# Attention visits, loads and inner factors moved within the slots of a paired attention-and-MLP kernel

## The chip, the cores and the metric

The kernel runs on one core of a Trainium2 chip. The metric is device time in microseconds (us), the median of several executions. Before the change it is 1418.35 us (three runs, 1418.15 to 1419.4). The engines are called as in the profile: PE (TensorE: matrix products), PEld (its weight loads), DVE (VectorE), ACT (ScalarE), POOL (GpSimd), SP (the queue from which all DMAs of the main part are issued).

## The reference

What is computed, cut to what matters:

```python
# 8 batches, 12 heads, 448 rows, 64 columns a head
q_n, k_n = rmsnorm(q, g_q), rmsnorm(k, g_k)
scores = q_n @ k_n.T / sqrt(64)
attn = exp(scores - max) ; attn = attn / (sum(attn) + 1e-9)
x = (attn @ v)                # to (8*448, 768)
h = x @ w_in                  # w_in 768 x 2048
g = h - tanh(h)
out = g @ w_out               # w_out 2048 x 768
```

All is float32 in the kernel's matrix products.

## The kernel before, in words

Attention is cut into 48 steps: a step s is one pair of heads of one batch, so a batch has six steps. The MLP is cut by batch. Both of its layers are multiplied in Strassen's manner (seven products in place of eight), so there are sums before and after the products; the seven are called p (or q, one level further in) and stand in the order 1, 5, 6, 2, 3, 7, 4. From batch 2 on, two batches make a pair: the first hidden layer of the pair (28 products of six matmuls), two "outer products" of the output layer, the second hidden layer, five more outer products. An outer product is itself seven inner products q of four matmuls with 224 columns, and a last, large one of eight matmuls with 448 columns.

The order of all work is written out by hand; nothing reorders it. Each engine takes its instructions in the order of recording, and waits for other engines at semaphores. The MLP is a generator, `stream`, which records one matmul at a time with whatever follows a finished product. `run(ns)` lets the stream go on for a given nominal time (0.373 us for a matmul of 224 columns). `slot(s)` places one step's attention: first the **visit** (`visit`), a burst of small matmuls in which the values of step s and the scores of step s+1 alternate; then 14 **points** in `work`, with a fifteenth part of the slot's nominal time of MLP between each two. At the points stand what step s+1 needs before its visit (sums of the exponentials: `add`, `fold`, `gather`, `spread_sums`, `widen_sums`, `turn_sums`), what step s+2 needs (`scale_blocks`, `turn_blocks`), and what step s+3 needs (`square_blocks`, `norm_blocks`, `meet_blocks`). In a hidden layer a slot holds 42 matmuls. `AHEAD_NS` is the MLP work that the slots of batch 2 record beyond the end of the single layers; as later slots hold whole fractions of a layer, it fixes where all later visits stand behind a layer's end: 18 matmuls behind it.

What the steps of the prediction touch:

- Products go to three banks in turn (`mm_bank`); products 2, 3 and 7 add to the banks of 1, 5 and 6. A product can start when the bank's last content has been read by DVE or ACT: L898 (ACT, product 1), L900, L902, L910, L906/L907, L914 (DVE: products 5, 6, 3, 7, 4), L878 with L879 (tanh on ACT and the subtraction, product 2), in the outer products L1156 and L1162 (ACT), L1089 (DVE), and L1096 (ACT) for the large product.
- A tanh (L878) of products 3, 7 and 4 is recorded one product later (`late["todo"]`) and its subtraction (L879) goes to POOL.
- The inner factors `u` (`inner_sum`, L1040) are differences of blocks of g, formed on POOL. For the first outer product of each part they are recorded beside the hidden layer, at the products that `due_sums` names; for the others within the outer product before. `outer_sum` (L1032) forms the outer ones on DVE.
- `divide` (L751, L752, L756) stands at the end of a visit: ACT copies one half of the values, DVE adds the other and multiplies by the reciprocal sums. Then DVE has `add` (L595), `add_third` (L601), `add_last` (L608), `fold` (L705), `fold_rest` (L712), `scale_blocks` (L528), `turn_blocks` (L538, L542). ACT follows with g on kT (L543), `gather` (L720, two halves of four copies), the squares (L499), `widen_sums` (L735). POOL raises to -1/2 (`power_blocks`, L521) right after the visit, and forms the sums of x (`x_sums_later`, L787).
- The q and k rows of a step are loaded by eight DMAs (`load_blocks`, L495) into one of two buffers (`qk_nat`); `scale_blocks` is the buffer's last reader. v is loaded by four DMAs after a visit. Weights go through a ring of six tiles (`ring_load`), five ahead.
- The scores of a visit go to three other banks in turn, so the second wave of scores waits until the exponential p_last (L570), the first of the visit, has read its bank.

Of the kernel before, what the change touches and what calls it, by code (L numbers as in the profile page):

```python
# [21 lines left out]
ENGINE_NS = 2.4  # L22
# [122 lines left out]
def bounded_path(tc, ctx, q, k, v, moe_w_in, moe_w_out, out, g_col, ident, ones, half_ones, neg_half, early):  # L145
# [30 lines left out]
    HS = S // 2  # L176
    HC, HF = CD // 2, CF // 2
    SETS = CF // 4
# [28 lines left out]
    def bank_of(name):  # L207

        turns[name] += 1
        return banks[name][turns[name] % len(banks[name])]  # L210
# [6 lines left out]
    def qk_rows():  # L217
        return nat.tile([P, 4 * NCH * D], F32, name="qk_nat", bufs=2)
# [241 lines left out]
    def turn(s, tk, tq):  # L460

        rr, n = normed.pop(s), early["n"]
        kn = loaded.pop(("k", s))
        for c in range(NCH):
            nc.tensor.transpose(tk[:, c * P : (c + 1) * P], kn[:, c].rearrange("p h d -> p (h d)"), ident)
        kT = qkp.tile([P, S], F32, name="kT")
        nc.scalar.mul(kT, tk[:, :S], g_col)
        for c in range(NCH):
            nc.tensor.transpose(
                tq[:, c * CP : (c + 1) * CP], n[:, c].rearrange("p h d -> p (h d)"), ident[:CP, :CP]  # L470
            )
        qT = qkp.tile([P, S], F32, name="qT")
        nc.scalar.copy(out=qT, in_=tq[:, :S])
        turned[s] = rr, kT, qT
# [12 lines left out]
    def load_blocks(s):  # L487
        b, hp = steps[s]
        t = loaded["qk", s] = qk_rows()[:, : 2 * S].rearrange("p (i j d) -> p i j d", i=2, j=NJ)
        for i, src in enumerate((q, k)):  # L490
            for h in range(2):
                rows = src[b, 2 * hp + h].rearrange("(j t) (m d) -> m t j d", t=BL, d=BL)
                for m in range(2):
                    r = (2 * h + m) * BL
                    nc.sync.dma_start(out=t[r : r + BL, i], in_=rows[m])  # L495

    def square_blocks(s):
        sq = normed["sq", s] = late["blocks"].tile([P, 2, NJ, BL], F32, name="qk_n", bufs=1)
        nc.scalar.activation(  # L499
            sq.rearrange("p i j d -> p (i j d)"), loaded["qk", s].rearrange("p i j d -> p (i j d)"), AF.Square  # L500
        )
# [7 lines left out]
    def meet_blocks(s):  # L509

        mine, other = normed["rr", s]
        for g in range(P // BL):
            own, met = slice(g * BL, (g + 1) * BL), slice((g ^ 1) * BL, ((g ^ 1) + 1) * BL)
            nc.vector.tensor_tensor(out=other[own], in0=mine[own], in1=mine[met], op=ALU.add)  # L514
        nc.vector.tensor_scalar(out=other, in0=other, scalar1=1.0 / D, scalar2=1e-6, op0=ALU.mult, op1=ALU.add)  # L515
        normed["rr", s] = other
# [16 lines left out]
    def turn_blocks(s, i):  # L533

        n = normed[s][:, i].rearrange("p j d -> p (j d)")
        if i == 0:
            qT = qkp.tile([P, S], F32, name="qT")
            nc.vector.transpose(out=qT, in_=n)  # L538
            turned[s] = qT
            return  # L540
        kT = qkp.tile([P, S], F32, name="kT")
        nc.vector.transpose(out=kT, in_=n)  # L542
        nc.scalar.mul(kT, kT, g_col)  # L543
        turned[s] = None, kT, turned[s]
        del normed[s]

    def sc_bank():
        return bank_of("sc")
# [34 lines left out]
    def full(s):  # L583

        return probs[s, 0][:, :, 0], probs[s, 1][:, :, 1], probs[s, 2][:, :, 0]

    def add(s, now=True):

        if s <= NP + NP // 2:
            sums[s] = []  # L590
            return
        t = early["sum"]
        sums[s] = [t]
        p = full(s)
        nc.vector.tensor_tensor(out=t, in0=p[0], in1=p[1], op=ALU.add)  # L595
        if now:
            add_third(s)
# [5 lines left out]
    def add_last(s):  # L603
        last = probs[s, KF][:, :, 0]
        for n in range(2 if sums[s] else 0):
            t = sums[s][0]
            part = t[n * KR : (n + 1) * KR, :, n * HS : (n + 1) * HS]
            nc.vector.tensor_tensor(out=part, in0=part, in1=last[n * KR : (n + 1) * KR], op=ALU.add)  # L608
# [107 lines left out]
    def gather(s, h):  # L716

        acc, part = whole[s], whole["part", s]
        for g in range(P // BL):
            nc.scalar.copy(  # L720
                out=acc[h * BL : (h + 1) * BL, g], in_=part[g * BL : (g + 1) * BL, h * NJ : (h + 1) * NJ]
            )

    def spread_sums(s):

        acc = whole[s]
        total = whole[s] = late["blocks"].tile([2 * BL, NJ], F32, name="sum_all")
        nc.vector.reduce_sum(total, acc.rearrange("p g j -> p j g"), axis=AX.X)
        nc.vector.reciprocal(total, total)

    def widen_sums(s):

        total = whole[s]
        wide = whole[s] = late["blocks"].tile([2 * BL, NJ, BL], F32, name="sum_w")
        nc.scalar.copy(out=wide, in_=total[:, :, None].to_broadcast([2 * BL, NJ, BL]))  # L735
# [33 lines left out]
    def x_sums_later(s, second):  # L769
        b, hp = steps[s]  # L770
        for c in {(HC + 1, 1): (0,), (HC + 1, 2): (1,), (HC + 2, 0): (2,)}.get((hp, second), ()):
            x_sums(b, (c,), range(4), nc.gpsimd)
# [82 lines left out]
    def hidden(b):  # L855
# [25 lines left out]
        def done_with(j):  # L881
# [11 lines left out]
            def use(p, bank):  # L893
                v = view(bank)
                if b >= PAIRED:
                    beside_hidden(b, j, p)
# [145 lines left out]
    def beside_hidden(b, j, p):  # L1042

        second = b % 2
        if second:
            due_sums = {(SETS // 2, 6): (0,), (SETS - 1, 4): (1,)}
        else:
            due_sums = {(SETS // 2, 6): (0,), (SETS - 1, 7): (1,), (SETS - 1, 4): (2, 3)}
        for i in due_sums.get((j, p), ()):
            inner_sum(3 if second else 1, i)  # L1050
        if second and j and p in (1, 6):
            outer_sum(p // 6, j - 1)
# [243 lines left out]

    H_NS = 4 * HS / ENGINE_NS * 7 * 6 * SETS
    O_NS = 4 * HS / ENGINE_NS * 7 * HC * HF
    AHEAD_NS = 4 * HS / ENGINE_NS * 18
    OUTER_NS = 4 * HS / ENGINE_NS * (7 * HF // 2 + 2 * HF)  # L1300

    def gap_ns(s):
# [3 lines left out]
        if s < 3 * NP:  # L1306
            return (H_NS + O_NS + AHEAD_NS) / (4 * NP)
        n = (s - 3 * NP) % (2 * NP)
        return (H_NS / 16, OUTER_NS * SOON / 8, H_NS / 16, OUTER_NS * (len(OUTER) - SOON) / 8)[(n > 3) + (n > 5) + (n > 9)]

    def has(s):
        return 0 <= s < NS
# [69 lines left out]
    def slot(s):  # L1382

        gap = gap_ns(s)
        av = av_banks
        if has(s + 1):
            scores(s + 1, KF)
        if s < FOLDED:
            last_values(s, av)
            totals(s, sc_bank())  # L1390
            divide(s, values(s, av))
            for c in range(KF):
                scores(s + 1, c)
        else:
            visit(s, av)
        if has(s + 2):
            load(s + 2, "v")
        rows, ahead, following = has(s + 2), has(s + 3), has(s + 1)
        folded = following and s + 1 >= FOLDED
        first = s + 3 == TURNED  # L1400
        scaled = rows and not first
        if scaled:
            power_blocks(s + 2)
        work = (
            ((following, lambda: add(s + 1, False)), (first, lambda: turn(s + 2, sc_bank(), sc_bank()))),
            (
                (following, lambda: add_third(s + 1)), (first, lambda: load_blocks(s + 3)),
                (True, lambda: x_sums_later(s, 0)),
            ),
            ((following, lambda: add_last(s + 1)), (first, lambda: load_blocks(s + 4))),  # L1410
            ((folded, lambda: fold(s + 1)),),
            ((folded, lambda: fold_rest(s + 1)), (True, lambda: x_sums_later(s, 1))),
            ((scaled, lambda: scale_blocks(s + 2)),),
            ((scaled, lambda: turn_blocks(s + 2, 0)), (folded, lambda: gather(s + 1, 0))),
            ((scaled, lambda: turn_blocks(s + 2, 1)), (folded, lambda: gather(s + 1, 1))),
            ((folded, lambda: spread_sums(s + 1)), (ahead, lambda: square_blocks(s + 3))),
            (
                (has(s + 4) and not first, lambda: load_blocks(s + 4)), (True, lambda: x_sums_later(s, 2)),
                (folded, lambda: widen_sums(s + 1)),
            ),  # L1420
            ((ahead, lambda: norm_blocks(s + 3)),),
            ((ahead, lambda: meet_blocks(s + 3)),),
            ((folded, lambda: turn_sums(s + 1)),),
            (),
        )
        for point in work:
            run(4 * gap / (len(work) + 1))
            for wanted, fn in point:
                if wanted:
                    fn()  # L1430
        run(4 * gap / (len(work) + 1))
# [10 lines left out]
    for s in range(2 * NP, NS):  # L1442
        slot(s)
# [346 lines left out]
```

## Time and profile before

| what | value |
|---|---|
| median of three runs | 1418.35 us |
| profiled execution | 1419.13 us, span 1417.3 us |
| busy: PE / DVE / POOL / ACT | 1338.8 / 1063.2 / 720.1 / 525.6 us |
| mean granted PE clock | 0.98 |
| a visit, and the time between two visits in a hidden layer | 5.50 us and 16.02 us |
| bytes read and written in HBM | 205 and 46 MB |

A span is the time from the first to the last instruction. A row of a timeline gives start, duration, engine, line, operation, result and operands, and in brackets the engine's idle time before it with what ended it. In a table of windows the columns are the window, its length, the busy time of PE, PEld, DVE, ACT and POOL with the number of instructions, the granted PE clock, the share of the DMA engines and GB/s. PE works on two records a matmul, so six matmuls are twelve records.

### The profile page before, as it was taken

How to read it: one execution, taken by the hardware profiler on the slowest of the kernel's cores; microseconds unless marked ns; L12 is line 12 of the kernel's file. 1: busy time of each engine (PE TensorE's matmuls, PEld its weight loads, DVE VectorE, ACT ScalarE, POOL GpSimd, SP SyncE). 2: the span in 40 equal slices, each digit the busy share in tenths (PEclk: the TensorE clock that was granted, in tenths of full speed). 3: DMA queues.
4: the chain of work that ended last, by engine and by line, in shares of the span. 5: the costliest groups of instructions: out<-in, count | busy, mean ns of one | idle time of the engine just before them, and what ended most of it. 6: DMA issues, size and time to landing. Idle time of an engine off the chain costs nothing.

```text
span 1417.3 us, 29026 instructions
## 1 busy us (share of the span) xinstructions
PE 1338.8 (94%) x11336; PEld 1044.0 (74%) x11336; DVE 1063.2 (75%) x1558; ACT 525.6 (37%) x1194; POOL 720.1 (51%) x409
## 2 busy tenths in 40 slices
PE   7988999999999997999899998899899999899996
PEld 3467844498889885688677896578777798689885
DVE  4999989668747888689788588689888688633564
ACT  7856555333333533344211444234412244301100
POOL 4756665257652447334774236624487224712651
PEclk9999999999999998999999999999999999999998
DMA  7878889889997654566455856365644775345554
GB/s 173 194 204 255 265 232 251 242 269 323 303 272 224 172 152 117 112 173 173 112 143 138 207 143 166 88 147 171 170 116 127 149 190 169 107 132 177 165 148 84
DMA packets 371685, 253.52 MB, mean 179 GB/s; under 512 B 282196, under 2 KB 310228, under 8 KB 371540
## 3 DMA queue, kind: packets, MB, share of 16 engines
q1 hardware_dynamic: 371536, 251.57, 65.2%
q8 instruction: 92, 1.51, 0.4%
q14 instruction: 53, 0.43, 0.1%
q10 hardware_dynamic: 4, 0.00, 0.0%
HBM read 205.23 MB, written 46.27 MB: 177 GB/s over the span
## 4 chain that ended last, share of the span: by engine, by line
PE 71%; DVE 14%; POOL 5%; issue 3%; DMA 3%; SPq 1%; ACT 1%; ACTq 0%; DVEq 0%; POOLq 0%
PE mm L831 32%; PE mm L1082 17%; PE sc L564 8%; PE mm L1246 5%; PE sc L630 5%; POOL u L1040 2%; DVE xT L756 1%; PE sc L668 1%; DVE qk_n L528 1%; PE sc L618 1%; POOL tt L787 1%; DVE rows L601 1%; DVE rows L608 1%; POOL rr_other L521 1%; DVE gT L1032 1%
## 5 line engine op out<-in xcount | busy, mean ns | idle before, releaser
L831 PE MATMUL mm<-xT,w_f 128*128 128x224 f32 x1296 | 265.9, 355 | 0.9 <-DVE s L900 0.9
L831 PEld LDWEIGHTS mm<-xT,w_f 128*128 128x128 f32 x1296 | 243.0, 190 | 21.0 <-issue 10.6
L564 PE MATMUL sc<-qT,kT 64*32 64x448 f32 (+1 forms) x3072 | 214.1, 500 | 3.1 <-ACT p_last L570 1.9
L521 POOL TENSOR_TENSOR rr_other<-rr_other,neg_half 128x28 f32<-128x28 f32 x33 | 160.6, 4868 | 102.8 <-DVE rr_other L515 102.8
L831 PE MATMUL mm<-tt,w_f 128*128 128x224 f32 x1044 | 208.0, 353 | 2.9 <-DVE acc L1089 2.7
L831 PEld LDWEIGHTS mm<-tt,w_f 128*128 128x128 f32 x1044 | 197.1, 190 | 5.1 <-DVE acc L1089 3.4
L1082 PE MATMUL mm<-u,w_f 128*128 128x224 f32 x672 | 146.5, 372 | 35.5 <-issue 16.7
L879 POOL TENSOR_TENSOR gT<-s,th 128x448 f32<-128x448 f32 x60 | 75.0, 1250 | 199.2 <-ACT th L878 199.2
L1082 PEld LDWEIGHTS mm<-u,w_f 128*128 128x128 f32 x672 | 132.6, 200 | 42.5 <-issue 26.7
L1082 PE MATMUL mm<-gT,w_f 128*128 128x224 f32 (+1 forms) x480 | 138.4, 442 | 2.1 <-ACT s L1156 2.1
L1082 PEld LDWEIGHTS mm<-gT,w_f 128*128 128x128 f32 x480 | 94.6, 199 | 42.6 <-issue 38.6
L564 PEld LDWEIGHTS sc<-qT,kT 64*32 64x32 f32 x3072 | 70.8, 106 | 70.8 <-issue 51.7
L879 POOL TENSOR_TENSOR g<-s,th 128x448 f32<-128x448 f32 x36 | 47.2, 1317 | 148.9 <-ACT th L878 140.9
L630 PE MATMUL sc<-p,v_nat 64*32 64x448 f32 x1120 | 111.4, 536 | 0.0
L1082 PE MATMUL mm<-g,w_f 128*128 128x224 f32 (+1 forms) x360 | 103.1, 439 | 3.5 <-DVE s L1089 3.0
L720 ACT COPY sum_g<-sum 32x14 f32<-32x14 f32 x280 | 56.3, 201 | 121.2 <-DVE sum L712 115.6
L878 ACT ACTIVATE th<-s 128x448 f32<-128x448 f32 x96 | 55.1, 575 | 120.0 <-DVE s L910 95.1
L1082 PEld LDWEIGHTS mm<-g,w_f 128*128 128x128 f32 x360 | 69.9, 197 | 34.0 <-issue 27.8
L752 DVE TENSOR_TENSOR xT<-xT,sc 128x448 f32<-128x448 f32 x32 | 19.8, 620 | 100.1 <-PE sc L564 79.3
L570 ACT ACTIVATE p<-sc 128x448 f32<-128x448 f32 x132 | 71.9, 545 | 50.6 <-PE sc L564 37.8
L1246 PE MATMUL mm<-gT,w_out 128*128 128x448 f32 x192 | 74.3, 542 | 0.0
L514 DVE TENSOR_TENSOR rr_other<-rr_mine 32x28 f32<-32x28 f32 x132 | 70.5, 534 | 3.9
(187 smaller groups left out, 2402.3 us busy)
## 6 DMA issues: line engine op xcount, KB each, us to landing
w_f<-w_in SPq DMA_DIRECT2D x196, 384.0 KB, 3.7
w_f<-w_inner SPq DMA_DIRECT2D x63, 512.0 KB, 3.6
w_f<-w_out SPq DMA_DIRECT2D x42, 512.0 KB, 4.6
w_raw<-in_moe_w_out_dram SPq DMA_DIRECT2D x16, 768.0 KB, 5.4
w_in<-w_out SPq DMA_DIRECT2D x21, 384.0 KB, 5.0
qk_nat<-in_q_dram SPq DMA_DIRECT2D x132, 56.0 KB, 2.2
qk_nat<-in_k_dram SPq DMA_DIRECT2D x132, 56.0 KB, 2.3
g<-w_out SPq DMA_DIRECT2D x14, 512.0 KB, 5.2
```

What stands on the lines that cost most here:

```text
L514: nc.vector.tensor_tensor(out=other[own], in0=mine[own], in1=mine[met], op=ALU.add)
L521: nc.gpsimd.tensor_tensor(out=mine, in0=mine, in1=neg_half[:, :1].to_broadcast([P, 2 * NJ]), op=ALU.pow)
L564: nc.tensor.matmul(tiles[h][i * BL : (i + 1) * BL, :n], lhsT=kT[r, c * P + at : c * P + at + BL], rhs=qT[r, first : first + n], start=True ...
L570: nc.scalar.activation(p[:, h, c if c < 2 else 0, :], tiles[h][:, :n], AF.Exp, scale=1.0 if rr is None else rr[:, 0, 2 * c + h : 2 * c + h ...
L630: nc.tensor.matmul(av[g][i * BL : (i + 1) * BL, :S], lhsT=v_nat[keys, h, c, m * BL : (m + 1) * BL], rhs=p[keys, h], start=first, stop=True ...
L720: nc.scalar.copy(out=acc[h * BL : (h + 1) * BL, g], in_=part[g * BL : (g + 1) * BL, h * NJ : (h + 1) * NJ])
L831: nc.tensor.matmul(bank[:, f * HS : (f + 1) * HS], lhsT=w[:, c * width + f, :], rhs=moving[p](c), start=(first and f == 0 and c == 0), sto ...
L878: nc.scalar.activation(th, h, AF.Tanh, bias=0.0, scale=1.0)
L879: eng.tensor_tensor(out=g[:, rows, cols], in0=h, in1=th, op=ALU.subtract)
L1040: nc.gpsimd.tensor_tensor(out=u, in0=a, in1=z, op=ALU.subtract)
L1082: nc.tensor.matmul(bank[:, :n], lhsT=w(i), rhs=mv, start=(first and i == 0), stop=(i == len(moving) - 1), skip_group_check=not first,)
L1246: nc.tensor.matmul(bank[:, :S], lhsT=w_out_row(f, n // HC)[:, n % HC * P : (n % HC + 1) * P], rhs=g[:, f, :], start=(f == 0), stop=(f == C ...
```

## The change

Four things move; no instruction is added, and none is removed.

1. `AHEAD_NS` holds 8 matmuls in place of 18: all visits from step 18 on stand 10 matmuls nearer to the layers' ends, and so do their points.
2. The q and k loads: in place of step s+4 at the tenth point of slot s, step s+3 at the first point.
3. In a pair's first hidden layer the second inner factor of the first outer product is recorded with the last two, at the last product (4), in place of the one before (7).
4. The two gathers go one point later each, `widen_sums` two points later, and `x_sums_later(s, 2)` stays at the tenth point.

```diff
-            due_sums = {(SETS // 2, 6): (0,), (SETS - 1, 7): (1,), (SETS - 1, 4): (2, 3)}
+            due_sums = {(SETS // 2, 6): (0,), (SETS - 1, 4): (1, 2, 3)}
...
-    AHEAD_NS = 4 * HS / ENGINE_NS * 18
+    AHEAD_NS = 4 * HS / ENGINE_NS * 8
...
-            ((following, lambda: add(s + 1, False)), (first, lambda: turn(s + 2, sc_bank(), sc_bank()))),
+            (
+                (following, lambda: add(s + 1, False)), (first, lambda: turn(s + 2, sc_bank(), sc_bank())),
+                (ahead and not first, lambda: load_blocks(s + 3)),
+            ),
...
-            ((following, lambda: add_last(s + 1)), (first, lambda: load_blocks(s + 4))),
+            ((following, lambda: add_last(s + 1)),),
...
-            ((scaled, lambda: turn_blocks(s + 2, 0)), (folded, lambda: gather(s + 1, 0))),
-            ((scaled, lambda: turn_blocks(s + 2, 1)), (folded, lambda: gather(s + 1, 1))),
-            ((folded, lambda: spread_sums(s + 1)), (ahead, lambda: square_blocks(s + 3))),
-            (
-                (has(s + 4) and not first, lambda: load_blocks(s + 4)), (True, lambda: x_sums_later(s, 2)),
-                (folded, lambda: widen_sums(s + 1)),
-            ),
+            ((scaled, lambda: turn_blocks(s + 2, 0)),),
+            ((folded, lambda: gather(s + 1, 0)), (scaled, lambda: turn_blocks(s + 2, 1))),
+            ((folded, lambda: gather(s + 1, 1)), (ahead, lambda: square_blocks(s + 3))),
+            ((folded, lambda: spread_sums(s + 1)), (True, lambda: x_sums_later(s, 2))),
             ((ahead, lambda: norm_blocks(s + 3)),),
-            ((ahead, lambda: meet_blocks(s + 3)),),
+            ((folded, lambda: widen_sums(s + 1)), (ahead, lambda: meet_blocks(s + 3))),
```

## The prediction

> **What bounds the kernel now.** I read the page first (PE, TensorE, busy 94% of the span), then the busy time by windows, then PE's waits from 450 to 1250 us, where the paired batches run beside attention, and last the timeline around the long waits.
>
> ```profile
> 450.00:1250.00 800.00, 756.26 (x6486) 601.17 (x6471) 632.18 (x923) 287.07 (x712) 401.88 (x208) 0.97 0.56 146
> 563.80:569.80 6.00, 5.97 (x18) 5.49 (x19) 2.39 (x9) 0.18 (x2) 4.31 (x1) 0.55 0.72 190
> 1250.00:1408.00 158.00, 155.72 (x727) 137.06 (x726) 79.99 (x114) 15.23 (x31) 62.98 (x35) 1.00 0.56 152
> ```
>
> The columns are busy time on PE, PEld, DVE, ACT, POOL, then the granted clock. PE is without work for 43.7 us of the 800. The second row is the stretch after one long wait: PE is busy at 0.55 of its clock, so (1 - 0.55) x 6.0 = 2.7 us more go. The last row is the end, without attention: nothing to win there.
>
> ```profile
> PE mm L1082 <- issue: 16.7, 3, 6.5
> PE mm L1082 <- POOL u L1040: 10.9, 2, 5.5
> PE mm L1082 <- DVE s L907: 7.0, 5, 2.1
> PE mm L831 <- DVE acc L1089: 2.7, 2, 1.4
> PE mm L1082 <- ACT s L1156: 2.1, 2, 1.9
> ```
>
> These are PE's waits in the same stretch: total, times, longest. They stand at the layers' ends. Three follow the end of a pair's first hidden layer (528.3, 867.9, 1208.9: 2.1 us each; the second pair adds 1.9), three the first two outer products (6.5, 6.5, 3.7), two the second hidden layer (5.5, 5.4), two the start of that layer (1.35, 1.3). After the eight longest the clock is down: windows of 6 us give 0.72 four times and 0.51 to 0.55 four times, 4 x 1.7 + 11.3 = 18 us. Waits and clock, some 61 us, are the ceiling.
>
> The longest wait in the timeline:
>
> ```profile
> 547.16 3.00 DVE L601 TENSOR_TENSOR rows<-rows,p_full 128x896 f32<-128x896 f32 x1
> 550.68 4.33 DVE L608 TENSOR_TENSOR rows<-rows,p_last 64x448 f32<-64x448 f32 x2
> 549.16 2.94 POOL L1040 TENSOR_TENSOR u<-gT 128x896 f32<-128x896 f32 x1
> 552.06 2.46 POOL L1040 TENSOR_TENSOR u<-gT,u 128x896 f32<-128x896 f32 x1
> 560.30 0.67 ACT L543 ACTIVATE kT<-kT,g_col 128x448 f32<-128x448 f32 x1 [1.77 <-DVE kT L542]
> 563.21 0.52 ACT L1096 COPY acc<-mm 128x448 f32<-128x448 f32 x1
> 563.83 1.08 PE L1082 MATMUL mm<-u,w_f 128*128 128x224 f32 x2 [6.50 <-issue]
> 526.28 2.94 DVE L528 TENSOR_TENSOR qk_n<-qk_nat,rr_other 128x896 f32<-128x896 f32 x1
> 530.43 1.37 PE L1082 MATMUL mm<-u,w_f 128*128 128x224 f32 x6 [2.12 <-DVE s L907]
> 679.00 1.80 POOL L879 TENSOR_TENSOR g<-s,th 128x448 f32<-128x448 f32 x1 [5.68 <-ACT th L878]
> 683.00 1.49 PE L1082 MATMUL mm<-u,w_f 128*128 128x224 f32 x3 [5.46 <-POOL u L1040]
> ```
>
> DVE's sums after a visit, 1.08 and 2 x 0.64 us in a quiet slot, take 3.00 and 4.33 beside POOL's inner factors. DVE is then late with kT (L542), ACT waits for it in its queue, and behind it stand the gathers, the squares and L1096, which empties the bank that PE's q=6 needs. "issue" hides this: PE starts 0.1 us after L1096 ends. At 528 scaling (L528, else 1.08) takes 2.94 beside POOL's factor, and L906/L907, behind it, empty PE's bank late. At 677 a tanh stands behind kT and the gathers on ACT, then its shrink and the second factor on POOL.
>
> **Visits 10 matmuls earlier.** A matmul of the stream takes 0.381 us (42 in the 16.02 us between two visits), a visit 5.50 us of PE. At a layer's end the visit now falls between q=5 and q=6. The products that waited at 557, 590 and 677 thus stand behind 5.5 us of other PE work, while the queue that they waited for starts 3.8 us sooner: 9.3 us of cover against 6.5, 1.35 and 5.5. The wait at 873 (L1156 after squares and widening on ACT) is covered alike. I count all of these as gone.
>
> **Factors later.** In the first layer u1 leaves the middle of DVE's burst (q=7) for the last use, where three factors of 2.1 us follow each other. L528 goes back to 1.08, L907 ends 1.9 us sooner, and the burst itself stands 3.8 us earlier: the waits of 2.1 are gone.
>
> First pair: 2.1 + 1.7 clock, 6.5 + 2.7, 1.35, 5.5 + 2.8: 22.7 us. Second: 22.7 + 1.9 + about 1 clock = 25.6. Third: 2.1 + 1.7 + 3.7 + 1.7 = 9.2. Together 57.5. The 1.0 us at 734 and 1075 stay.
>
> What is late next, from visits' ends on, with the durations of the quiet slot at 496 to 508 us (sixteen DVE instructions, 11.3 us up to L542; the same number after the change):
>
> - First hidden layer, j=2: u0 stays at q=6, but this is now 10 matmuls after the visit, in the burst. A DVE instruction waits 1.9 us; L902 and L879 are then late by 0.2 to 0.5, and the next visit's second wave by 1.0. 1.5 x 3 pairs = 4.5.
> - First outer product: shrinks to about 17.4 us after the last visit's end, then u1 to u3 to 23.7. The next visit ends at 21.5, so L756 waits for u3, one shrink (1.1) slips between, and q=5's L1089, now behind the visit in DVE's order, ends 4.9 us after the visit. q=3 needs its bank after 3.05: 1.85. The large product waits 1.0 for q=3's sum behind L705. 2.85 x 3 = 8.6.
> - Second outer product: 0.5 x 2, from the x sums on POOL beside L595 and L601 (1.41, 1.36 instead of 1.09).
> - Second hidden layer: its outer sum (1.02) moves from ahead of the visit into the burst. ACT then reaches the exponential p_last 2.2 us after a visit starts (now 0.75), ends it at 2.55, and the second wave of scores needs its bank at 1.9: 0.65 x 3 visits x 2 pairs = 3.9.
> - Third outer product: u3 is recorded behind the power (L521, 4.78 us), where it stood ahead: about 1.0 x 2.
>
> In all 20; one half-clock window in some places brings it to 23.5.
>
> [...] By the rows alone (L756 at 0.62) q=3 would wait 0 to 0.7, 4 us less in all. [...] Here waits of 2.12 and 1.88 were enough (0.72 in the next 6 us), 1.35 was not. [...]
>
> **Loads.** Eight DMAs of 0.5 us issue move on SP from point 10, where SP stood up to 11.1 us for scaling to free the buffer (547.64 to 559.13), to point 1 behind the four v loads, ahead of the weight loads. The buffer is then free since the slot before, so SP no longer waits; the 6 us of issue fall in the visit, where no weights are used, and five weight tiles are loaded ahead (over 7.5 us of products). Squares at point 9 come over 10 us later, against 2.2 us of landing. Zero; without that cover ACT would wait at L499, with tanhs and copies behind it: up to 2 us a slot.
>
> **Gathers and widening later.** One point and two points, 1.07 us each; DVE's L728 waits for the gathers, and rs_T (L741), which waits for widening, is used at the next visit's end, 3.5 us after it. Zero, or 0.5 us a slot, inside the fourth item.
>
> Net 57.5 - 23.5 = 34 us. The profiled execution took 1419.13 (span 1417.3): 1385. The median of the runs shown is 0.8 lower: **1384 us**.
>
> **Rivals.**
> (a) The cover is half as good: DVE stays about 4 us behind at the layers' ends, and half of the waits reappear one product later with the half clock. For it: DVE is busy 18.05 of 20.6 us around 528. Against: visits give PE 5.5 us without DVE's help. 57.5/2 - 23.5 = 5, up to 22 with my costs overrated: 1396 to 1413.
> (b) My new waits don't come (the row of L756 decides, u0 hides): gain 48 to 58, 1360 to 1370.
> (c) Slower: ACT's queue ahead of a visit. L543, gathers, squares, three tanhs, widening and the copy L898 (4.9 us) all stand between kT and p_last. 20 visits in the hidden layers hang on it, each at its full lateness. The slack is 0.8 us now (p_last ends 1.1 after a start, needed at 1.9). Up to 0.65 late costs what I counted; from 1.7 us on in each of 20 visits it eats the 34. At 2.5 it is 50 lost, 1434. Against: DVE's order up to L542 is as long as before.
> (d) Nothing: waits only move from q=6 to q=3, within 3 us of 1418.
>
> **Chances.** My forecast 55% (its own range 1370 to 1396), (a) 21%, (b) 8%, (d) 3%, (c) 13%. The range 1362 to 1412 holds the forecast, nearly all of (a) and most of (b), and reaches no further. A measurement tells 0.2% (2.8 us) from no change: faster 0.84, same 0.03, slower 0.13.
>
> **What would show it.** PE's waits of 6.5, 5.5 and 2.1 us at L1082 gone, total under 25 us; L1096 still late, but beneath a visit; L528 near 1.1 at the first layer's end; new waits of 1 to 2 us for L1089 at q=3; SP without its wait at L495. I am wrong if the distance between hidden-layer visits grows from 21.5 to over 23 us, with p_last more than 3 us after their start, or if L499 waits for a load.

## The result and the profile after

| | before | after |
|---|---|---|
| median of five runs | 1419.4 us (1418.15 to 1419.57) | 1407.82 us (1404.12 to 1409.74) |
| profiled execution, span | 1419.13 us, 1417.3 us | 1407.51 us, 1405.4 us |

The ratio is 0.9919 (95% interval 0.9903 to 0.9935). The change is faster by 0.8%, clear of noise. The forecast was 1384 us, a gain of 34 us. The gain is a third of that: the time lies outside the forecast's own range of 1370 to 1396 us, and inside the wider one, which was drawn around rival (a) as well.

The same two views as before, of the changed kernel: windows, and PE's waits from 450 to 1250 us.

```profile
450.00:1250.00 800.00, 770.00 (x6473) 615.07 (x6472) 645.97 (x934) 282.07 (x706) 410.53 (x211) 0.98 0.58 149
540.80:546.80 6.00, 6.00 (x24) 5.68 (x24) 5.93 (x5) 0.00 (x0) 5.92 (x3) 0.74 0.19 57
```

```profile
PE mm L1082 <- DVE acc L1089: 18.3, 9, 2.7
PE mm L1082 <- DVE s L1089: 8.0, 4, 3.5
PE mm L831 <- DVE s L902: 1.7, 2, 0.9
PE sc L564 <- ACT p_last L570: 1.7, 2, 0.9
```

Of the five waits that the prediction shows, none is among them: "issue" (L1096's bank), the factor `u`, L907, L1156 and the one of L831 for L1089 are gone, as forecast. In their place stand waits of L1082 for the sums of the inner products (L1089), which were 0.5 and 3.0 us in all before. PE is idle for 30.0 us of the 800 instead of 43.7. The second row of the windows shows a granted clock of 0.74 in the 6 us after the first new wait.

The place that decides most, the first outer product of the first pair, in the timeline: start, duration, then the instruction. The visit here lasts from 529.31 to 534.81 us.

```profile
529.52 7.33 DVE L514 TENSOR_TENSOR rr_other<-rr_mine 32x28 f32<-32x28 f32 x4
536.89 1.05 DVE L515 TENSOR_SCALAR rr_other<-rr_other 128x28 f32<-128x28 f32 x1
539.02 1.27 DVE L756 TENSOR_TENSOR xT<-xT,rs_T 64x448 f32<-64x448 f32 x2
540.32 0.39 DVE L1089 TENSOR_TENSOR acc<-mm,s 128x224 f32<-128x224 f32 x1
543.05 4.81 DVE L608 TENSOR_TENSOR rows<-rows,p_last 64x448 f32<-64x448 f32 x2
530.59 2.12 POOL L1040 TENSOR_TENSOR u<-gT,u 128x896 f32<-128x896 f32 x1
532.66 2.12 POOL L1040 TENSOR_TENSOR u<-gT 128x896 f32<-128x896 f32 x1
534.73 2.08 POOL L1040 TENSOR_TENSOR u<-gT,u 128x896 f32<-128x896 f32 x1
540.77 3.33 PE L1082 MATMUL mm<-gT,w_f 128*128 128x224 f32 x8 [2.73 <-DVE acc L1089]
549.34 4.23 PE L1082 MATMUL mm<-gT,w_f 128*128 128x448 f32 x7 [2.22 <-DVE acc L1089]
```

Four additions of 0.18 us each take 7.33 us: each ends 0.04 to 0.05 us after a subtraction on POOL, the first after L879's (530.63), the others after the three factors (532.71, 534.78 and 536.81). L515 takes 1.05 instead of 0.18. So DVE reaches the divide 3.6 us after the visit's end (L752 at 538.42, the visit ended at 534.81), q=5's sum stands behind it, and PE waits 2.73 at q=3. L608 then takes 4.81 instead of 1.27 beside the next two factors, and PE waits 2.22 for q=3's sum before the large product.

### The profile page after: what moved, and what is told of

It reads as the page before. It is cut to its first block, busy times and chain, and to the rows that moved or that the text cites. A ratio compares the mean times of both kernels' runs of the same rounds, so it can differ in the third digit from the quotient of the medians.

```text
span 1405.4 us, 29010 instructions
## 1 busy us (share of the span) xinstructions
PE 1341.7 (95%) x11336; PEld 1048.9 (75%) x11336; DVE 1077.7 (77%) x1558; ACT 523.3 (37%) x1194; POOL 727.2 (52%) x409
## 4 chain that ended last, share of the span: by engine, by line
PE 71%; DVE 17%; DMA 4%; issue 3%; SPq 2%; ACT 1%; POOL 1%; ACTq 0%; DVEq 0%; POOLq 0%
PE mm L831 34%; PE mm L1082 17%; PE sc L564 8%; PE mm L1246 5%; PE sc L630 5%; DVE rr_other L514 2%; DVE rows L608 2%; DMA w_f<-w_in 1%; DMA gT<-in_moe_w_in_dram 1%; DVE acc L1089 1%; PE sc L668 1%; DVE g L1032 1%; DVE xT L756 1%; PE sc L618 1%; DVE rows L601 1%
## 5 line engine op out<-in xcount | busy, mean ns | idle before, releaser
L831 PE MATMUL mm<-xT,w_f 128*128 128x224 f32 x1296 | 264.3, 353 | 1.7 <-DVE s L902 1.7
L831 PEld LDWEIGHTS mm<-xT,w_f 128*128 128x128 f32 x1296 | 244.4, 190 | 8.2 <-issue 4.3
L564 PE MATMUL sc<-qT,kT 64*32 64x448 f32 (+1 forms) x3072 | 217.8, 500 | 4.3 <-ACT p_last L570 3.1
L831 PE MATMUL mm<-tt,w_f 128*128 128x224 f32 x1044 | 213.3, 355 | 0.4
L521 POOL TENSOR_TENSOR rr_other<-rr_other,neg_half 128x28 f32<-128x28 f32 x33 | 166.8, 5056 | 83.8 <-DVE rr_other L515 83.2
L831 PEld LDWEIGHTS mm<-tt,w_f 128*128 128x128 f32 x1044 | 195.2, 190 | 17.7 <-issue 15.4
L879 POOL TENSOR_TENSOR gT<-s,th 128x448 f32<-128x448 f32 x60 | 73.3, 1236 | 201.3 <-ACT th L878 199.4
L1082 PE MATMUL mm<-gT,w_f 128*128 128x224 f32 (+1 forms) x480 | 138.6, 443 | 13.7 <-DVE acc L1089 12.6
L1082 PE MATMUL mm<-u,w_f 128*128 128x224 f32 x672 | 139.8, 360 | 1.3 <-DVE acc L1089 1.3
L1082 PEld LDWEIGHTS mm<-u,w_f 128*128 128x128 f32 x672 | 130.0, 195 | 8.6 <-issue 4.5
L1082 PEld LDWEIGHTS mm<-gT,w_f 128*128 128x128 f32 x480 | 92.9, 196 | 53.7 <-issue 36.2
L879 POOL TENSOR_TENSOR g<-s,th 128x448 f32<-128x448 f32 x36 | 43.3, 1216 | 165.8 <-ACT th L878 150.4
L630 PE MATMUL sc<-p,v_nat 64*32 64x448 f32 x1120 | 119.4, 537 | 0.0
L1082 PE MATMUL mm<-g,w_f 128*128 128x224 f32 (+1 forms) x360 | 104.2, 443 | 11.5 <-DVE s L1089 6.9
L1082 PEld LDWEIGHTS mm<-g,w_f 128*128 128x128 f32 x360 | 70.4, 197 | 39.8 <-issue 26.0
L752 DVE TENSOR_TENSOR xT<-xT,sc 128x448 f32<-128x448 f32 x32 | 19.7, 617 | 101.2 <-PE sc L564 58.5
L514 DVE TENSOR_TENSOR rr_other<-rr_mine 32x28 f32<-32x28 f32 x132 | 80.2, 607 | 3.8
L878 ACT ACTIVATE th<-s 128x448 f32<-128x448 f32 x96 | 53.1, 571 | 54.4 <-DVE s L910 16.7
```

Source lines behind the costliest of these rows:

```text
L521: nc.gpsimd.tensor_tensor(out=mine, in0=mine, in1=neg_half[:, :1].to_broadcast([P, 2 * NJ]), op=ALU.pow)
L564: nc.tensor.matmul(tiles[h][i * BL : (i + 1) * BL, :n], lhsT=kT[r, c * P + at : c * P + at + BL], rhs=qT[r, first : first + n], start=True ...
L630: nc.tensor.matmul(av[g][i * BL : (i + 1) * BL, :S], lhsT=v_nat[keys, h, c, m * BL : (m + 1) * BL], rhs=p[keys, h], start=first, stop=True ...
L831: nc.tensor.matmul(bank[:, f * HS : (f + 1) * HS], lhsT=w[:, c * width + f, :], rhs=moving[p](c), start=(first and f == 0 and c == 0), sto ...
L878: nc.scalar.activation(th, h, AF.Tanh, bias=0.0, scale=1.0)
L879: eng.tensor_tensor(out=g[:, rows, cols], in0=h, in1=th, op=ALU.subtract)
```

## The experiments

Theory 1: where the visits stand is the gain, since a wait that lies beneath a visit costs nothing; the rest was given back because DVE's instructions are held up beside POOL's in places where no visit covers it. Theory 2: the gathers and widening, later on ACT, cost what is missing. Theory 3: the gain is SP's, which no longer waits for the buffer of q and k; where visits stand doesn't matter. Each ratio below is to the kernel before, measured anew beside each variant, with its 95% interval; the change has 0.9919 (0.9903 to 0.9935). Where two times in us are close, the ratios are the better comparison.

### Visits back at 18 matmuls

```diff
-    AHEAD_NS = 4 * HS / ENGINE_NS * 8
+    AHEAD_NS = 4 * HS / ENGINE_NS * 18
```

> The change with its visits put back to 18 matmuls behind a layer's end; loads, factors, gathers and widening stay as in the change. Theory 1 (the visits' cover is the gain; DVE instructions held up beside POOL took most of it back in new places): the waits of 5 to 6.5 us at L1082 return, the new ones at q=3 and in the visits go, 1411 to 1420 us. Theory 2 (the later gathers and widening on ACT cost what is missing): slower than before, 1420 to 1430. Theory 3 (the gain is SP's, freed from its wait for the q and k buffer; where the visits stand is of no weight): 1404 to 1410, as the change.

1420.21 us, 1.0012 (0.9997 to 1.0028): the whole gain is gone. PE's waits in the same window:

```profile
PE mm L1082 <- POOL u L1040: 20.4, 5, 4.7
PE mm L1082 <- issue: 12.1, 2, 6.0
```

The waits at the layers' ends are back. With the factors' new place and the visits' old one the first of them is longer: PE waits for the second factor, and 3.65 us where it waited 2.1 before.

```profile
530.73 1.70 PE L1082 MATMUL mm<-u,w_f 128*128 128x224 f32 x7 [3.65 <-POOL u L1040]
```

### The visit shift alone

The line above, reversed, in the kernel before.

> The kernel before with the visits at 8 matmuls alone. Theory 1: it has most of the change's gain, 1403 to 1412. Theory 2: it has more than the change, 1385 to 1400, since gathers and widening stand where they stood. Theory 3: within 3 us of 1419, and SP still waits about 11 us at L495.

1412.73 us, 0.995 (0.9934 to 0.9967). A good half of the change's gain comes from the visits alone, which speaks for theory 1 and against theory 2. PE has a new wait that the change doesn't have:

```profile
PE mm L831 <- DVE s L907: 7.7, 9, 1.1
```

The next run but one shows where it comes from.

### Loads as before

```diff
-                (ahead and not first, lambda: load_blocks(s + 3)),
...
-            ((folded, lambda: spread_sums(s + 1)), (True, lambda: x_sums_later(s, 2))),
+            (
+                (has(s + 4) and not first, lambda: load_blocks(s + 4)), (folded, lambda: spread_sums(s + 1)),
+                (True, lambda: x_sums_later(s, 2)),
+            ),
```

> The change with q and k loaded at the tenth point, one step further ahead, as before. Theory 1: within 3 us of the change, 1405 to 1411. Theory 3: 1415 to 1420.

(At the one step with `first` a load goes back too, not shown.) 1408.38 us, 0.992 (0.9901 to 0.9939), as the change. SP's waits for the buffer, 74.1 us in the kernel before and none in the change, are back:

```profile
SPq L495 <- DVE qk_n L528: 94.7, 20, 10.4
```

94.7 us of waiting on SP, none of it visible in the time: theory 3 falls, and the forecast's zero for the loads stands.

### Gathers and widening as before

```diff
-            ((scaled, lambda: turn_blocks(s + 2, 0)),),
-            ((folded, lambda: gather(s + 1, 0)), (scaled, lambda: turn_blocks(s + 2, 1))),
-            ((folded, lambda: gather(s + 1, 1)), (ahead, lambda: square_blocks(s + 3))),
-            ((folded, lambda: spread_sums(s + 1)), (True, lambda: x_sums_later(s, 2))),
+            ((scaled, lambda: turn_blocks(s + 2, 0)), (folded, lambda: gather(s + 1, 0))),
+            ((scaled, lambda: turn_blocks(s + 2, 1)), (folded, lambda: gather(s + 1, 1))),
+            ((folded, lambda: spread_sums(s + 1)), (ahead, lambda: square_blocks(s + 3))),
+            ((True, lambda: x_sums_later(s, 2)), (folded, lambda: widen_sums(s + 1))),
...
-            ((folded, lambda: widen_sums(s + 1)), (ahead, lambda: meet_blocks(s + 3))),
+            ((ahead, lambda: meet_blocks(s + 3)),),
```

> The change with the gathers and the widening at the points where they stood before. Theory 1: within 4 us of the change (1404 to 1412). Theory 2: the visits of the second hidden layer go back from 6.0 to 7.2 us to 5.5, and the time falls to 1385 to 1400.

1414.3 us, 0.9973 (0.9959 to 0.9988). Both theories missed: this part of the change is worth a gain of 0.5%. DVE's timeline of this kernel, around the end of a set (seven products) in the hidden layer:

```profile
505.01 0.62 DVE L542 STREAM_TRANSPOSE kT<-qk_n 128x448 f32<-128x448 f32 x1
507.27 0.24 DVE L728 TENSOR_REDUCE sum_all<-sum_g 64x14 f32<-64x56 f32 x1 [1.64 <-ACT sum_g L720]
507.70 0.55 DVE L906 TENSOR_TENSOR s<-mm,s 128x448 f32<-128x448 f32 x1
```

The reduction L728 (`spread_sums`) is recorded ahead of L906 and L907 here. It waits 1.64 us for ACT's gathers, and the two that empty PE's bank wait behind it: PE waits up to 1.08 us for L907 at the end of a hidden set and 12.3 us in all from 450 to 1250 us, where it doesn't wait for L907 in the change. There L728 stands one point later, behind L907. In the kernel before it stood behind L907 too (L907 at 506.31 us); the visits' move alone brings it ahead, as the run with nothing but that move showed.

### The gathers alone as before

The two gathers go back; L728 and `widen_sums` stay late.

```diff
-            ((scaled, lambda: turn_blocks(s + 2, 0)),),
-            ((folded, lambda: gather(s + 1, 0)), (scaled, lambda: turn_blocks(s + 2, 1))),
-            ((folded, lambda: gather(s + 1, 1)), (ahead, lambda: square_blocks(s + 3))),
+            ((scaled, lambda: turn_blocks(s + 2, 0)), (folded, lambda: gather(s + 1, 0))),
+            ((scaled, lambda: turn_blocks(s + 2, 1)), (folded, lambda: gather(s + 1, 1))),
+            ((ahead, lambda: square_blocks(s + 3)),),
```

> The change with the gathers alone at the points where they stood before; the reduction that reads them (L728) and the widening stay late. If the gathers' place on ACT is what was worth 6 us: 1412 to 1416. If it is the place of L728 on DVE, which waits 1.6 us for the gathers with L906 and L907 behind it: as the change, 1404 to 1410.

1408.3 us, 0.9941 (0.9918 to 0.9964). The interval overlaps the change's and, by a little, that of the run above, so the time alone doesn't decide. DVE's timeline does:

```profile
480.11 0.58 DVE L906 TENSOR_TENSOR s<-mm,s 128x448 f32<-128x448 f32 x1
480.62 0.61 DVE L907 TENSOR_TENSOR s<-mm,s 128x448 f32<-128x448 f32 x1
481.82 0.24 DVE L728 TENSOR_REDUCE sum_all<-sum_g 64x14 f32<-64x56 f32 x1 [0.60 <-ACT sum_g L720]
```

L907 is ahead again, L728's wait of 0.60 has neither of the two sums behind it, and PE has no wait for L907 left from 450 to 1250 us. So what counts for these waits is that the reduction stands behind the two sums, rather than ACT's copies. `widen_sums` stays late in this run too; a cost of its place on ACT isn't told apart.

### The second factor back at product 7

```diff
-            due_sums = {(SETS // 2, 6): (0,), (SETS - 1, 4): (1, 2, 3)}
+            due_sums = {(SETS // 2, 6): (0,), (SETS - 1, 7): (1,), (SETS - 1, 4): (2, 3)}
```

> The change with the second factor of the first outer product back at product 7 of the last hidden set. Prediction's own step: the wait of 2.1 at q=5 returns in each pair, 1411 to 1416. Theory 1 (contention in new places): the burst at product 7 is delayed by about 2 us, but the factors end 2 us earlier before the visit's end, so the wait at q=3 shrinks from 2.7 to about 1: within 4 us of the change, 1403 to 1411.

1404.62 us, 0.9906 (0.9885 to 0.9927): the same as the change within the intervals. The wait of 2.1 us doesn't come back; the one at q=3 of the first outer product falls from 2.73 to 1.77. With the visits moved, the factors' move is not needed.

### Sums recorded before the stream hands over

In the change the stream hands over after an inner product's last matmul, ahead of its sum. The edit lets it hand over behind the sum.

```diff
-                yield 4 * n / ENGINE_NS
+                if i < len(moving) - 1:
+                    yield 4 * n / ENGINE_NS
...
+        took = 4 * HS / ENGINE_NS
...
                 at(k, q)
+                yield took
...
             late["todo"].append(lambda p=p, v=bank[:, :S]: combine_outer(p, HC - 1, v))
+            yield 2 * took
```

> The change, with the stream handing over after an inner product's sums are recorded, not before: the sum of q=5 (L1089) stands ahead of the visit's divide on DVE, and the last factor of the third outer product ahead of POOL's power. Theory 1: the waits at q=3 fall from 2.7 and 2.3 to under 1, with their half clock: 1396 to 1404. If the order of that one sum isn't the cause (DVE is late as a whole), within 2 us of the change.

1399.16 us, 0.9866 (0.9841 to 0.9891), 0.5% better than the change.

```profile
536.94 0.34 DVE L1090 TENSOR_TENSOR acc<-mm,s 128x224 f32<-128x224 f32 x1
537.22 0.59 DVE L752 TENSOR_TENSOR xT<-xT,sc 128x448 f32<-128x448 f32 x1
537.34 1.78 PE L1082 MATMUL mm<-gT,w_f 128*128 128x224 f32 x8 [0.78 <-DVE acc L1090]
```

q=5's sum (L1089, here L1090) is ahead of the divide. The wait at q=3 of the first outer product falls from 2.73 to 0.78, and in the third from 2.30 to 1.80. But new ones come in: PE's idle time from 450 to 1250 us is 30.9 us, against 30.0 in the change. What fell are the stretches of 3.4 us at half clock there, from eight to two; the granted clock over the 800 us is 1.00 against 0.98. The gain is thus mainly the clock's: about the same idle time, in shorter pieces. The edit also puts the third outer product's last factor ahead of POOL's power; this run doesn't tell the two apart.

### One addition instead of four

It leaves out the exchange between the two halves of a row's squares.

```diff
-        for g in range(P // BL):
-            own, met = slice(g * BL, (g + 1) * BL), slice((g ^ 1) * BL, ((g ^ 1) + 1) * BL)
-            nc.vector.tensor_tensor(out=other[own], in0=mine[own], in1=mine[met], op=ALU.add)
+        nc.vector.tensor_tensor(out=other, in0=mine, in1=mine, op=ALU.add)
```

> The change with one DVE addition in place of the four that add the other half's squares (L514). It leaves out the exchange between the halves, so each half row is scaled by its own squares. The busy time saved is 3 x 0.18 us a slot. Theory 1 (each two-input instruction waits for one of POOL's): in the outer products the four take 4.1 and 3.4 us beside factors; one takes 1 to 2; the waits at q=3 fall by about 2 us and the one at 721 us by 2 to 3: 1390 to 1401. If DVE is late through its own work alone, 1404 to 1408.

1398.69 us, 0.9859 (0.9835 to 0.9882). By DVE's own busy time the edit is worth 0.54 us a slot, on an engine that is busy for 646 of the 800 us, against 770 for PE; it gives 0.6%. The wait at q=3 of the first outer product falls from 2.73 to 1.21 and the one before the large product from 2.22 to 0.22, 3.5 us together, and the stretches at half clock from eight to three (granted clock over the 800 us 0.99). The run also bears on two steps of the forecast, in timeline and waits:

```profile
535.30 3.25 DVE L754 TENSOR_TENSOR xT<-xT,rs_T 64x448 f32<-64x448 f32 x2
538.58 0.39 DVE L1087 TENSOR_TENSOR acc<-mm,s 128x224 f32<-128x224 f32 x1
```

```profile
PE mm L1080 <- POOL u L1038: 5.9, 2, 3.0
```

(Lines stand two lower in this kernel: L754 is L756.) The divide's multiplications take 3.25 instead of 1.27 beside the last factor and the subtraction behind it. That is the step that the forecast had for L756; in the change itself DVE comes too late for it. And in the third outer product PE now does wait for the factor behind the power, 3.0 us, where the forecast had 1.0.

### The first factor earlier

```diff
-            due_sums = {(SETS // 2, 6): (0,), ...
+            due_sums = {(SETS // 2, 1): (0,), ...
```

(The rest of the line stays.) In both hidden layers.

> The change with the first factor of each hidden layer at product 1 instead of product 6 of its third set, as far ahead of the visit as it stood in the kernel before. Theory 1: the visits behind it go back from 6.44 to 5.5 us in the first hidden layer, and in the second the wait for L902 goes: 3 x 1.1 + 2 x 2.4 = 8 us, 1398 to 1403. If these visits are long through ACT's queue alone, within 2 us of the change.

1402.16 us, 0.9887 (0.9862 to 0.9912); against the change the intervals overlap, so the time alone doesn't settle it. The trace shows the mechanism: the visits behind this factor in the first hidden layer are 5.50 us long again instead of 6.44, and the wait for L902 falls from 1.7 to 0.4 in all. In the second hidden layer the visits stay at 6.0 to 7.3.

### The last three together, with the second factor at product 7

Sums first, first factor at product 1, second factor at product 7: the edits shown above.

> The change with three edits together: sums recorded before the stream hands over, the first factor at product 1, the second back at product 7. Alone they gave about 8.6, 5.7 and 3.2 us against the change. Theory 1 with separate places of contention: they add up, 1389 to 1394. If they take away the same wait, 1396 to 1400.

1388.91 us, 0.9798 (0.978 to 0.9815). They add up: by the ratios 1.2% better than the change, where the three alone gave 0.5, 0.3 and 0.1%. PE's idle time from 450 to 1250 us is 27.1 us, against 30.0 in the change, but no stretch at half clock is left of the eight; the execution's mean granted clock is 0.995 against 0.985.

### And the exchange on ACT

```diff
-            nc.vector.tensor_tensor(out=other[own], in0=mine[own], in1=mine[met], op=ALU.add)
+            nc.scalar.copy(out=other[own], in_=mine[met])
+        nc.vector.tensor_tensor(out=other, in0=other, in1=mine, op=ALU.add)
```

> The same three edits, and the exchange of the halves' squares by four copies on ACT and one addition on DVE, in place of four two-input additions on DVE. Theory 1: most of the 9 us that one addition gave comes on top, less what four copies (0.9 us) cost in ACT's queue ahead of a visit: 1382 to 1391. If ACT's queue is the limit there (visits over 6.5 us in both hidden layers), slower than without: 1394 to 1402.

1381.27 us, 0.9744 (0.9726 to 0.9761): 2.6% faster than the kernel before, and the whole computation. PE's waits from 440 to 1220 us, and the window:

```profile
PE mm L1083 <- DVE acc L1091: 8.5, 6, 1.8
PE sc L565 <- ACT p_last L571: 2.7, 8, 0.4
PE mm L1083 <- DVE s L1091: 2.2, 2, 1.1
```

```profile
440.00:1220.00 780.00, 763.66 (x6602) 613.64 (x6601) 598.64 (x855) 307.63 (x823) 411.03 (x212) 1.00 0.60 154
```

No wait is longer than 1.8 us, and the clock is nowhere halved there. The copies have a price in ACT's queue: the visits of the first pair's second hidden layer are 6.63 to 6.86 us long, against 5.51 to 6.43 in the run above.

### The same with visits at 18

> The fastest of the variants so far (three edits and the exchange on ACT) with its visits put back to 18 matmuls behind a layer's end. Theory 1: the cover of the visits goes, waits of 3 to 6 us return at the layers' ends: 1396 to 1410. If the relief of DVE alone made these variants fast, within 4 us of 1381.

1399.08 us, 0.9881 (0.9856 to 0.9906). The edit is the one of the first run.

```profile
PE mm L1083 <- issue: 12.1, 2, 6.0
PE mm L1083 <- POOL u L1041: 7.8, 2, 3.9
PE mm L1083 <- DVE s L908: 7.0, 5, 2.1
```

The three waits of the kernel before are back, in good part (12.1, 7.8 and 7.0 us here; 16.7, 10.9 and 7.0 there), and with them eight stretches at half clock (0.98 from 450 to 1250 us). With less contention the visits' place is worth 1.4% (0.9744 against 0.9881), against 0.9% in the change (0.9919 against 1.0012). Without the visits' move all the rest gives 1.2%. So DVE's relief and the visits' cover are two gains, and both together give more (2.6%) than their sum.

## Why the prediction was right and wrong

**Right: visits as cover.** The forecast's 48.3 us for the first two pairs did come in: each of the waits that it listed is gone from the trace, and they come back with the visits at 18. Taken from visit to visit (first visit of the first pair's hidden layer to that of the third's) the stretch is 680.60 us before and 671.65 after, 8.95 less. The forecast had 48.3 - 17.9 = 30.4 there. The table below leaves 48.3 - 45.5 = 2.8 of it. Ten waits of 0.11 to 0.45 us, 3.1 us in all, which I hadn't listed, went too. Some 3 us are not accounted for by this count.

**Right: loads at nothing.** Shown by the run with the loads put back.

**Wrong: the step "What is late next".** This is the step that failed. It named nearly every place, but its sum for the first two pairs was 17.9 us, and the profile shows 45.5; in part the path was another than the one it followed.

| term | forecast | profile after |
|---|---|---|
| first factor beside the burst, first hidden layer | 3.0 | 2.2 |
| first outer product | 5.7 | 9.6 (2.7 + 2.6 at q=3, 2.2 + 2.1 before the large one) |
| second outer product | 1.0 | 1.1 |
| second hidden layer (longer visits, L902; from visit to visit) | 3.9 | 11.3 |
| third outer product | 2.0 | 9.4 (2.3 at q=3 and 3.4 later, twice, less 2.1 that stood there before) |
| half clock | 2.3 | 11.9 (seven windows of 3.4 us at half) |
| sum | 17.9 | 45.5 |

Three things made the terms too small. First, I followed the contention with POOL for the long instructions (L756, L608) and not for the four short ones (L514), as if an instruction of 0.18 us could cost only that. Beside a row of factors the four took 1.15, 2.04, 2.05 and 2.00 us, 7.33 us together. With L515 behind them they took 8.41 us at 529.52, and in the third outer product 6.51 at 675.70 and 5.36 at 718.92, instead of about 1.0. So the first outer product's path was another: L756, which I had waiting for the last factor, ran undisturbed (1.27), because DVE had lost its time ahead of it, in L514 and L515. The run with one addition shows that as a cause: three additions left out, 0.54 us of DVE's own time, take 3.5 us from the two waits of the first outer product. That L756 would be held up was an estimate; a trace shows it even before the change, 3.10 us for its two multiplications beside a factor at 695.98, which the 0.62 of the prediction leaves out. The kernel before had the same burst already, partly beneath a visit, and I didn't read it:

```profile
536.02 6.07 DVE L514 TENSOR_TENSOR rr_other<-rr_mine 32x28 f32<-32x28 f32 x4
```

Second, ACT's queue ahead of a visit in the second hidden layer. I had p_last 2.2 us after a visit's start; the profile after has, for the visit that starts at 605.01:

```profile
603.67 0.56 ACT L878 ACTIVATE th<-s 128x448 f32<-128x448 f32 x1
605.48 0.58 ACT L878 ACTIVATE th<-s 128x448 f32<-128x448 f32 x1 [1.25 <-POOL g L879]
607.31 0.58 ACT L878 ACTIVATE th<-s 128x448 f32<-128x448 f32 x1 [0.80 <-POOL g L879]
608.20 0.61 ACT L570 ACTIVATE p_last<-sc 128x224 f32<-128x224 f32 x2
```

3.2 us, and the visit is 7.21 us long. The next two visits have p_last 2.2 and 2.4 us after their start and are 0.7 and 0.9 us longer than 5.50, close to the 0.65 that I had for each. The tanhs have two buffers (the pool's `bufs=2`), and they are now close together: the later ones wait for POOL's subtractions, which I left out of the chain. That the buffers are the cause is read from these waits alone; no run has a third one. This was rival (c)'s mechanism, in the second hidden layers alone, and the forecast's own sign of being wrong showed there: visits 23.2 and 23.8 us apart, and one p_last more than 3 us after a visit's start.

Third, the clock. I put 3.5 us for all three pairs (23.5 less 20), an estimate that no run shows. Nine waits of 2.06 to 3.46 us brought eight stretches of 3.4 us at half clock, and these cost 13.3 us, half of PE's busy time in them. The last section has these stretches.

**Wrong: "Factors later".** The waits of 2.1 us are gone through the visits. With the visits at 18 the wait is longer with the factors late (3.65) than with the second one back at product 7 (2.13, in the last run), and in the change taking the move back costs nothing that can be measured (0.9906 against 0.9919).

**Wrong: "Gathers and widening later" at 0, or 0.5 us a slot.** I followed the copies on ACT and left out the place of the reduction L728, which moves a point too. Where it stands ahead of L907, PE waits for its bank up to 1.08 us at the end of a hidden set; the part is worth 0.5%.

**Rivals.** (a), cover half as good, has the right time and half of the reason. DVE did come about 4 us late (3.6), and waits with half clock did stand a little later, at q=3. But the listed waits were covered in full, and DVE was late through L514 beside the factors, which (a) didn't have. (b) and (d) fell; (c) came in part, as told.

## What to carry to other kernels

Before a piece of work is moved, list for each engine what is recorded right behind it and ahead of the next result that the bound engine needs: what follows a product recorded ahead of a divide, or one reduction behind two sums, was worth 0.5% here without any work saved. Price a burst of short DVE instructions by the POOL subtractions that run beside it (four additions of 0.18 us took 7.33 us here), and give it to ACT or merge it. Look at the length of each wait and not only at the sum: the nine of 2.06 to 3.46 us here cost 13.3 us of clock as well. A long stretch of work that needs nothing from the slow engines is best placed where several late results come together (0.9744 against 0.9881 here), and then the next place has to be searched in the same way.

## What the runs showed of the hardware

- DVE beside POOL's subtractions, in the change from 450 to 1250 us: of the 108 additions L514 (two SBUF inputs) and the 27 instructions L515 (one SBUF input and constants), 81 took 0.17 to 0.18 us. The other 54 took 0.53 to 2.05 us, and each of them ended 0.03 to 0.05 us after a subtraction of POOL's (L879, L1040 or L787). Transposes (L705, 1.11 us at 696 us), reductions (L506, 1.07 at 714 us) and sums with a PSUM input (L1089, 0.38 at 550 us), each beside a factor, took no longer there: all 29 L705 took 1.10 to 1.11 us, all 27 L506 1.07 to 1.09, and the L1089 of 540.32, beside no factor, 0.39. All 46 multiplications L756 that lie within POOL's power (L521, 4.78 to 6.09 us) in the changed kernel took 0.62 us, as in a quiet slot.
- The granted clock in the change falls to 0.50 for stretches of 3.413 us. The eight from 450 to 1250 us start whole multiples of 3.413 us apart; the first four, at 540.52, 550.76, 687.29 and 724.84 us, 3, 40 and 11 times. Three such windows, the first two one behind the other:

```profile
537.11:540.52 3.41, 0.93 (x5) 0.57 (x4) 3.31 (x6) 0.35 (x1) 3.29 (x2) 1.00 0.41 100
540.52:543.93 3.41, 3.16 (x9) 2.87 (x10) 3.38 (x5) 0.00 (x0) 3.41 (x2) 0.50 0.13 54
881.85:885.26 3.41, 2.15 (x12) 1.80 (x10) 3.35 (x3) 0.00 (x0) 3.33 (x3) 1.00 0.23 42
```

  PE was idle for 2.48 us in the first, and the next is at half clock. The wait of 2.06 us before 886.06 lies in two stretches, 1.26 us of idle time in the first of them, and no half clock follows. In the traces before and after, with the time from 450 to 1250 us divided into windows of 3.413 us in step with these stretches, 16 windows at full clock were followed by one at half, and PE was idle for 1.88 us or more in each; 430 were not, with 1.72 us or less in all but one (2.00). And with the sums recorded first, 30.9 us of idle time came with two stretches at half clock, where 30.0 us came with eight in the change.
- 94.7 us of waiting on SP, with the loads put back, cost nothing that could be measured (0.992 against 0.9919), and PE waited for no weight tile from 450 to 1250 us in that run.
